# The division of the softmax rows moves from GpSimd to VectorE and ScalarE

## The chip, the core and the metric

One core of a Trainium2 chip runs the whole program. The metric is device microseconds of one execution. Engines are named as the profile names them: PE is TensorE's matrix multiply and PEld its weight load, DVE is VectorE, ACT is ScalarE, POOL is GpSimd, SP is SyncE, whose queue issues nearly all DMAs.

## The reference: causal attention, then two feed-forward layers

```python
scores = scale * np.matmul(q, k.transpose(0, 1, 3, 2))      # q, k, v: 2 x 12 x 448 x 64
scores = np.where(mask, -1000000000.0, scores)              # causal mask
scores = scores - np.max(scores, axis=-1, keepdims=True)
attn = np.exp(scores)
attn = attn / (np.sum(attn, axis=-1, keepdims=True) + 1e-09)
x = np.matmul(attn, v)                                      # -> 896 tokens x 768
h = x @ w_in1;  g = h * np.clip(h + 3.0, 0.0, 6.0) / 6.0;   x = g @ w_out1
h = x @ w_in2;  g = P(h) / (Q(h) + 1e-06);                  out = g @ w_out2
```

P is a cubic with coefficients a, Q is quadratic in |h| with coefficients b; the hidden width is 2048.

## The kernel before

**Attention stage.** The 24 heads are worked as 12 pairs: a pair is two heads of one batch, on the two halves of the 128 partitions. The 448 queries are cut into seven row blocks of 64, r = 0 to 6, and block r needs only (r + 1) * 64 columns of scores, so 1792 columns a pair. For each pair, in this order:

- *load, scores*: DMA of q and k, then 14 fp32 matmuls into four PSUM banks (line 427).
- *max*: DVE adds the mask and writes the scores to SBUF tile `e{r}` while it reduces the row extreme into `stat` (line 439, one per block).
- *exp*: ACT, in place on `e{r}`, with the row sum as accumulator (line 446).
- *bias, reciprocal*: DVE or ACT adds 1e-9 to the sums (lines 456 and 458), DVE takes the reciprocal (line 462). This is done for two parts of a pair: blocks 6, 5, 0 and blocks 4, 3, 2, 1.
- *norm*: `e{r}` is multiplied in place by its row's reciprocal (`a_norm`, lines 465 to 470). Before, GpSimd does all 84 of them.
- *transpose*: four groups of four 128x128 blocks of `e`, on PE with the identity, into one PSUM bank a group (line 476). A group needs the norms of the blocks it holds.
- *move*: the transposed bank is copied to SBUF tile `et` by ACT or DVE (lines 326 and 328).
- *apply*: `et` times `v` on PE (line 496). Then *x hi* (ACT, line 326) and *x rest* (DVE, line 508) split the result into two fp32r parts for the layers.

There are two sets of `e` tiles (`EB = 2`), so the maxima of pair n + 2 wait for the transposes of pair n; six `et` tiles and three `v` tiles.

**Layers.** Every weight matrix comes as 64-bit words and is decoded in chunks of three 128x128 tiles: *magnitude* and *tail* on ACT (lines 610 and 616), *shift* and *sign* on DVE (620 and 626), *w hi* on ACT (326), *w rest* on DVE (644). The products (line 715) are three matmuls for each tile and batch, 128x448; there are 2304 of them. They may start when the last pair's scores are done, and each needs the pairs of its own rows of x, so the first products lie among the last pairs' transposes. Some chunks are decoded early, kept in DRAM and fetched again.

**What sets the order.** Nothing is reordered on the chip: each engine takes its instructions in the order in which the program was written out, and waits at the head of its queue. That order is made when the program is built, by the class `Program`. `add` files an operation with its due time, what it reads and writes, and a cost for each engine that may do it; `order` then takes again and again the operation and engine that could begin first (ties by due time) and books the cost on that engine. The costs are formulas such as `c_pool`; `DUE` shifts the due time by the kind of operation; `PAIR` is the distance of two pairs' due times; `STAY` puts off a change of PE's tiling. They move no data, but they decide the order on every engine and, where an operation lists two engines, which of them does it.

Of the kernel before, what the change touches and what calls it, by code (L numbers as in the profile page):

```python
# [35 lines left out]
class Program:  # L36
# [15 lines left out]

    TILING = {"scores": "quarters", "apply": "columns"}
    DRAIN = 0.16
    STAY = 5.83

    def __init__(self, rings, banks, due):
        self.rings, self.banks, self.due = rings, banks, due
# [2 lines left out]
    def add(self, kind, at, engines, fn, *args, reads=(), writes=(), new=()):  # L61

        self.ops.append((kind, at, engines, fn, args, tuple(reads), tuple(writes), tuple(new)))

    def order(self):
# [44 lines left out]
        while can:  # L112
            best = None
            for n, t in can.items():
# [20 lines left out]
                for e, cost in ops[n][2].items():  # L135
                    mine = max(t[e], free[e], room), due[n] + self.STAY * turn, n, e, cost
                    if best is None or mine < best:
# [46 lines left out]
def c_act(n):  # L184
    return 0.051 + n / 1200


def c_dve(n):
    return 0.068 + n / 960


def c_pool(n):
    return 0.15 + n * 0.0021


def c_pe(n, passes):
    return passes * (0.0025 + n / 2400)

# [5 lines left out]
def c_mm(n, passes):  # L204
# [2 lines left out]


DUE = {
    "load": -89.1,  # L210
    "keep": 0.0,
    "fetch": -20.0,
    "load v": -0.1,
    "norm": 4.2,
    "scores": 10.5,
    "max": -10.7,
    "exp": 31.3,
    "bias": 13.8,
    "reciprocal": -27.8,
    "transpose": -38.3,  # L220
    "move": 7.4,
    "apply": 15.3,
    "x hi": -25.6,
    "x rest": 70.4,
    "constants": -8.8,
    "w load": -84.1,
    "magnitude": -7.3,
    "tail": -30.5,
    "shift": 17.2,
    "sign": -12.6,  # L230
    "w hi": 79.6,
    "w rest": -29.6,
    "product": 0.0,
    "relu": 8.8,
    "gate": 1.1,
# [17 lines left out]
    "out": -3.6,  # L253
    "store": 7.5,
}
PAIR = 5.9


def plan(KM, KF):
# [17 lines left out]
def tile_attention_moe_moe2(  # L277
# [235 lines left out]
    for n in range(len(pairs)):  # L513
        t, last = PAIR * n, n == len(pairs) - 1
        for which in ("kr", "qr"):
            raw = which, n
            add(
                "load", t, {"act" if n == 0 and which == "qr" else "dma": 1.26}, qk_load, which, n,
                writes=[raw], new=[(which, raw)],
            )  # L520
        add(
            "load v", t, {"dma": 0.9}, v_load, n, reads=[("empty", n % VB)], writes=[("v", n)],
            new=[("v", ("v", n))],
        )
        sc = [("sc", n, held) for held in BANKS]
        add(
            "scores", t, {"pe": 1.7}, a_scores, n, reads=[("kr", n), ("qr", n)],
            writes=sc + ["scored"] * last, new=[("s", key) for key in sc],
        )
        for late, r in enumerate(order):  # L530
            w, first, mine = (r + 1) * CP, late == 0, next(held for held in BANKS if r in held)
            add(
                "max", t + late, {"dve": c_dve(w)}, a_max, n, r,
                reads=[("sc", n, mine), "masks"] + [("stat", n)] * (not first)
                + [("m", n, mine[0])] * (r != mine[0]),
                writes=[("e", n, r), ("st", n, r), ("m", n, r)] + [("stat", n)] * first,
                new=[(f"e{r}", ("e", n, r))] + [("stat", ("stat", n))] * first,
            )
            add(
                "exp", t + late, {"act": 0.235 + c_act(w)}, a_exp, n, r, reads=[("stat", n)],  # L540
                writes=[("e", n, r), ("st", n, r)],
            )
        for part, held in enumerate((STRAIGHT, SWAPPED)):
            add(
                "bias", t + 2 * part, {"act": 0.2, "dve": 0.1}, a_bias, n, part,
                reads=[("st", n, r) for r in held] + [("stat", n)], writes=[("r", n, part)],
            )
            add(
                "reciprocal", t + 2 * part, {"dve": 0.15}, a_recip, n, part, reads=[("stat", n)],
                writes=[("r", n, part)],  # L550
            )
            for r in held:
                w = (r + 1) * CP
                add(
                    "norm", t + 2 * part, {"pool": c_pool(w)}, a_norm, n, r,
                    reads=[("r", n, part), ("stat", n)], writes=[("e", n, r)],
                )
        for g, group in enumerate(GROUPS):
            add(
                "transpose", t + g, {"pe": 0.436}, a_transpose, n, g,  # L560
                reads=["masks", ("pads", n % EB)] + [("e", n, r) for r in sorted({r for r, _ in group})],
                writes=[("pt", n, g)], new=[("t", ("pt", n, g))],
            )
            add(
                "move", t + g, {"act": c_act(512), "dve": c_dve(512)}, a_move, n, g,
                reads=[("pt", n, g)], writes=[("et", n, g)], new=[("et", ("et", n, g))],
            )
        for a, gs_ in enumerate(APPLY):
            cols = 1024 * len(gs_) // len(GROUPS)
            add(  # L570
                "apply", t + 2 * a, {"pe": c_pe(cols, 4) + 0.1}, a_apply, n, a,
                reads=[("et", n, g) for g in gs_] + [("v", n)], writes=[("o", n)],
                new=[("o", ("o", n))] if a == 0 else (),
            )
        b, hp = pairs[n]
        add("x hi", t, {"act": c_act(S) + 0.04}, a_hi, n, reads=[("o", n)], writes=[("x", hp, b)])
        add("x rest", t, {"dve": c_dve(S)}, a_lo, n, reads=[("o", n)], writes=[("x", hp, b)])
# [22 lines left out]
    raw, full, tail, split = {}, {}, {}, {}  # L600
# [54 lines left out]

    base = PAIR * len(pairs) + 10

# [208 lines left out]
    t, i, every = base, 0, tuple(range(B))  # L866
# [6 lines left out]
    while i < len(chunks):  # L873

        side = chunks[i][0][0] == 2
        n = 1 if not side else 2 if chunks[i + 2][0][0] == 2 else 3
# [72 lines left out]
```

## Time and profile before

| | |
|---|---|
| runs of the kernel | 560.67 us, median of 3 (560.19 to 560.8) |
| the profiled execution | 560.22 us, of which the span in the trace is 558.4 us |
| PE busy | 538.7 us (96%) |
| DVE, ACT, POOL busy | 423.2, 397.9 and 82.2 us |
| granted TensorE clock, mean | 0.991 of full speed |

The span is the time from the first to the last instruction; the rest of the device time lies around it. A busy share is an average over two stages that have different limits: the attention stage is roughly the first 100 us, the layers are the rest. Times in the trace count from the start of the span.

### The profile page before, as it was taken

How to read it: one execution, taken by the hardware profiler on the slowest of the kernel's cores; microseconds unless marked ns; L12 is line 12 of the kernel's file. 1: busy time of each engine (PE TensorE's matmuls, PEld its weight loads, DVE VectorE, ACT ScalarE, POOL GpSimd, SP SyncE). 2: the span in 40 equal slices, each digit the busy share in tenths (PEclk: the TensorE clock that was granted, in tenths of full speed). 3: DMA queues.
4: the chain of work that ended last, by engine and by line, in shares of the span. 5: the costliest groups of instructions: out<-in, count | busy, mean ns of one | idle time of the engine just before them, and what ended most of it. 6: DMA issues, size and time to landing. Idle time of an engine off the chain costs nothing.

```text
span 558.4 us, 9410 instructions
## 1 busy us (share of the span) xinstructions
PE 538.7 (96%) x3236; PEld 492.8 (88%) x3236; DVE 423.2 (76%) x925; ACT 397.9 (71%) x882; POOL 82.2 (15%) x104
## 2 busy tenths in 40 slices
PE   6888887999999999999999999999999999999997
PEld 5766766999999999999999999999999999999996
DVE  3588784679999998777777349999989999975420
ACT  5798885579898987776776359788678778855410
POOL 3999978000000000000000000000000000000000
PEclk9699999999999999999999999999999999999999
DMA  5775141147778777777766342234324323336100
GB/s 163 219 202 166 43 119 58 54 146 213 249 253 242 258 231 279 258 252 242 243 236 223 136 137 85 86 94 165 110 85 136 118 86 103 124 112 188 61 33 33
DMA packets 39311, 87.12 MB, mean 156 GB/s; under 512 B 4704, under 2 KB 14688, under 8 KB 39264
## 3 DMA queue, kind: packets, MB, share of 16 engines
q1 hardware_dynamic: 39104, 86.30, 47.9%
q8 instruction: 25, 0.41, 0.3%
q10 hardware_dynamic: 160, 0.23, 0.1%
q14 instruction: 22, 0.18, 0.1%
HBM read 71.18 MB, written 15.34 MB: 155 GB/s over the span
## 4 chain that ended last, share of the span: by engine, by line
PE 85%; POOL 11%; DVE 2%; issue 1%; ACT 1%; POOLq 0%; DVEq 0%
PE bank L715 82%; POOL e L470 11%; DVE e L439 1%; PE bank L476 1%; PE bank L376 1%; PE bank L496 1%; PE bank L427 1%; ACT et L326 0%; DVE et L328 0%; POOLq L945 0%; ACT e L446 0%; ACT o L326 0%; DVE stat L462 0%; ACT tail L616 0%; POOL ident masks.py:199 0%
## 5 line engine op out<-in xcount | busy, mean ns | idle before, releaser
L715 PE MATMUL bank<-yh,w 128*128 128x448 f32 x384 | 112.0, 362 | 0.0
L715 PE MATMUL bank<-rh,w 128*128 128x448 f32 x384 | 97.2, 362 | 0.0
L715 PE MATMUL bank<-xh,w 128*128 128x448 f32 x384 | 93.7, 363 | 0.0
L715 PE MATMUL bank<-ph,w 128*128 128x448 f32 x384 | 92.6, 362 | 0.0
L644 DVE TENSOR_TENSOR w<-full,w 128x384 fp32r<-128x384 f32 x96 | 53.2, 555 | 46.0 <-ACT w L326 45.6
L326 ACT ACTIVATE w<-full 128x384 fp32r<-128x384 f32 x96 | 50.2, 523 | 51.6 <-PE bank L715 50.8
L616 ACT ACTIVATE tail<-raw 128x384 uint32<-128x384 uint8 x128 | 69.4, 554 | 23.0 <-DVE full L620 19.7
L610 ACT ACTIVATE full<-raw 128x384 f32<-128x384 f32 x128 | 68.9, 549 | 20.2 <-DVE w L644 19.1
L620 DVE SCALAR_TENSOR_TENSOR full<-full,tail 128x384 uint32<-128x384 uint32 x128 | 69.7, 555 | 17.3 <-ACT full L610 15.5
L470 POOL TENSOR_SCALAR e<-e,stat 128x448 f32<-128x448 f32 (+6 forms) x84 | 79.5, 971 | 12.2 <-DVE stat L462 8.4
L715 PEld LDWEIGHTS bank<-rh,w 128*128 128x128 f32 x384 | 71.9, 188 | 5.2 <-ACT qy L783 0.3
L715 PEld LDWEIGHTS bank<-yh,w 128*128 128x128 f32 x384 | 71.9, 187 | 5.1 <-DVE p L767 0.5
L715 PEld LDWEIGHTS bank<-ph,w 128*128 128x128 f32 x384 | 72.0, 188 | 4.6
L715 PEld LDWEIGHTS bank<-xh,w 128*128 128x128 f32 x384 | 71.7, 188 | 4.5
L626 DVE SCALAR_TENSOR_TENSOR full<-raw,full 128x384 uint32<-128x384 uint32 x128 | 69.5, 558 | 1.9
L715 PE MATMUL bank<-yl,w 128*128 128x448 f32 x192 | 69.6, 363 | 0.0
L715 PE MATMUL bank<-rl,w 128*128 128x448 f32 x192 | 54.3, 362 | 0.0
L715 PE MATMUL bank<-xl,w 128*128 128x448 f32 x192 | 53.8, 361 | 0.0
L715 PE MATMUL bank<-pl,w 128*128 128x448 f32 x192 | 53.8, 361 | 0.0
L446 ACT ACTIVATE e<-e,stat 128x448 f32<-128x448 f32 (+6 forms) x84 | 41.7, 503 | 7.7 <-DVE stat L439 7.2
L476 PE MATMUL bank<-ident,e 128*128 128x128 f32 x192 | 28.5, 295 | 15.0 <-POOL e L470 15.0
L476 PEld LDWEIGHTS bank<-ident,e 128*128 128x128 f32 x192 | 22.4, 149 | 22.6 <-POOL e L470 22.4
(56 smaller groups left out, 732.9 us busy)
## 6 DMA issues: line engine op xcount, KB each, us to landing
raw<-in_w SPq DMA_DIRECT2D x128, 384.0 KB, 3.5
kept<-ws SPq DMA_DIRECT2D x32, 384.0 KB, 4.1
w<-kept SPq DMA_DIRECT2D x32, 384.0 KB, 3.3
kr<-in_kT SPq DMA_DIRECT2D x24, 112.0 KB, 2.9
out_T<-o SPq DMA_DIRECT2D x12, 224.0 KB, 2.2
qr<-in_qT SPq DMA_DIRECT2D x22, 112.0 KB, 2.9
v<-in_v SPq DMA_DIRECT2D x12, 128.0 KB, 2.8
v<-in_v SPq DMA_DIRECT2D x12, 96.0 KB, 3.0
```

The lines of the kernel that those rows point to most:

```text
L326: e.activation(out, in_, AF.Copy)
L376: e.matmul(bank[banks[0]][:, :P], ident, ident, start=True, stop=True)
L427: e.matmul(tiles["sc", n, r][halves[slot]], q[halves[j], r * CP:w], k[halves[j], :w], start=True, stop=True,)
L446: e.activation(t, t, AF.Exp, bias=stat[:, 0, at_:at_ + 1], scale=-1.0, accum_out=stat[:, 1, at_:at_ + 1],)
L470: e.tensor_scalar(t, t, by, None, ALU.mult)
L476: e.transpose(to[:, x], es[n % EB][r][:, c * P:(c + 1) * P], ident)
L610: e.activation(full[i], high, AF.Copy, scale=TO_F32)
L616: e.activation(tail[i], top, AF.Copy, bias=-31.0 / 64.0, scale=1.0 / 32.0)
L620: e.scalar_tensor_tensor(bits, bits, 3, tail.pop(i), ALU.logical_shift_left, ALU.bitwise_or)
L626: e.scalar_tensor_tensor(bits, raw.pop(i)[:, :, :, 1], 0x80000000, bits, ALU.bitwise_and, ALU.bitwise_or)
L644: e.tensor_tensor(split[i][:, 1], full.pop(i), split[i][:, 0], ALU.subtract)
L715: e.matmul(sums[which, m, b], split[i][:, w, j, :], x, start=k == 0 and n == 0, stop=last and n == 2,)
```

## The change

The operation *norm* may now be done by DVE or ACT, whichever the planner finds free first, and no longer by POOL. POOL keeps the masks, the identity and the zeros at the start. `a_norm` itself had both forms already: `activation` with a per-row scale on ACT, `tensor_scalar` elsewhere. Two costs of PE operations, `STAY`, `PAIR` and most numbers of `DUE` are other values; two lines of that table are shown.

```diff
-    STAY = 5.83
+    STAY = 2.21
...
+def c_norm(n, r, w):
+    return {"dve": 0.07 + w / 1920, "act": 0.06 + w / 1200}
...
-    "load": -89.1,
+    "load": -129.6,
...
-    "norm": 4.2,
+    "norm": 10.4,
...
-PAIR = 5.9
+PAIR = 5.6
...
-            "scores", t, {"pe": 1.7}, a_scores, n, reads=[("kr", n), ("qr", n)],
+            "scores", t, {"pe": 1.42}, a_scores, n, reads=[("kr", n), ("qr", n)],
...
-                    "norm", t + 2 * part, {"pool": c_pool(w)}, a_norm, n, r,
+                    "norm", t + 2 * part, c_norm(n, r, w), a_norm, n, r,
...
-                "apply", t + 2 * a, {"pe": c_pe(cols, 4) + 0.1}, a_apply, n, a,
+                "apply", t + 2 * a, {"pe": c_pe(cols, 4) + 0.08}, a_apply, n, a,
```

In the changed kernel's file every line from 196 on stands four lines lower: the norms are lines 472 (ACT) and 474 (DVE) there, the transposes 480, the products 719.

Counted over the whole program, DVE gets 46 of the 84 norms (4, 6, 7, 7, 9, 5 and 8 of the widths 448, 384, 320, 256, 192, 128 and 64: 11,008 columns) and ACT gets 38 (8, 6, 5, 5, 3, 7 and 4: 10,496 columns). The moves go from 27 on ACT and 21 on DVE to 16 and 32, and the additions of 1e-9 from 14 on ACT and 10 on DVE to 5 and 19. Every other operation stays on its engine.

ACT's queue at the first two pairs; tiles `e_91` to `e_97` are blocks 0 to 6 of the first set (pair 0), `e_98` to `e_104` those of the second (pair 1), and `stat` holds a pair's row numbers. Before:

```order
L446 ACTIVATE e_94,stat_196<-e_94,stat_196 128x256
L456 ACTIVATE stat_196<-stat_196 128x3
L446 ACTIVATE e_104,stat_214<-e_104,stat_214 128x448
L446 ACTIVATE e_92,stat_196<-e_92,stat_196 128x128
L446 ACTIVATE e_98,stat_214<-e_98,stat_214 128x64
L446 ACTIVATE e_102,stat_214<-e_102,stat_214 128x320
L446 ACTIVATE e_100,stat_214<-e_100,stat_214 128x192
L446 ACTIVATE e_103,stat_214<-e_103,stat_214 128x384
```

The same place in the changed kernel:

```order
L450 ACTIVATE e_94,stat_193<-e_94,stat_193 128x256
L450 ACTIVATE e_104,stat_214<-e_104,stat_214 128x448
L450 ACTIVATE e_92,stat_193<-e_92,stat_193 128x128
L450 ACTIVATE e_98,stat_214<-e_98,stat_214 128x64
L450 ACTIVATE e_102,stat_214<-e_102,stat_214 128x320
L472 ACTIVATE e_96<-e_96,stat_193 128x384
L472 ACTIVATE e_94<-e_94,stat_193 128x256
L472 ACTIVATE e_92<-e_92,stat_193 128x128
L450 ACTIVATE e_100,stat_214<-e_100,stat_214 128x192
```

Three norms of pair 0 stand between the exponentials of pair 1, and the addition of 1e-9 has left for DVE. DVE's queue a little later, where pair 0 is normalised and pair 2's first maximum follows. Before:

```order
L439 ISA e_99,stat_214<-bank_73,mask 128x128
L439 ISA stat_214 128x1
L458 TENSOR_SCALAR stat_196<-stat_196 128x4
L462 RECIPROCAL stat_196<-stat_196 128x4
L458 TENSOR_SCALAR stat_214<-stat_214 128x3
L462 RECIPROCAL stat_214<-stat_214 128x3
L328 COPY et_0_276<-bank_78 128x512
L439 ISA e_97,stat_281<-bank_74,mask 128x448
```

The same place in the changed kernel:

```order
L443 ISA e_99,stat_214<-bank_73,mask 128x128
L443 ISA stat_214 128x1
L466 RECIPROCAL stat_193<-stat_193 128x3
L466 RECIPROCAL stat_193<-stat_193 128x4
L474 TENSOR_SCALAR e_97<-e_97,stat_193 128x448
L474 TENSOR_SCALAR e_91<-e_91,stat_193 128x64
L474 TENSOR_SCALAR e_95<-e_95,stat_193 128x320
L474 TENSOR_SCALAR e_93<-e_93,stat_193 128x192
L332 COPY et_0_272<-bank_78 128x512
L443 ISA e_97,stat_279<-bank_74,mask 128x448
```

Four norms now stand ahead of the first move and of pair 2's maxima. PE's queue at the end of the attention stage, from the last transposes (line 476, now 480) on. Before:

```order
L476 MATMUL bank_76<-ident,e_101 128x2x64
L476 MATMUL bank_76<-ident,e_102 128x2x64 x2
L715 MATMUL bank_73<-xh_82,w_867 128x448
L715 MATMUL bank_78<-xh_84,w_867 128x448
L715 MATMUL bank_73<-xl_83,w_867 128x448
L715 MATMUL bank_78<-xl_85,w_867 128x448
L715 MATMUL bank_73<-xh_82,w_867 128x448
L715 MATMUL bank_78<-xh_84,w_867 128x448
L496 MATMUL bank_80<-et_0_1286,v_107 64x128 x4
```

The same place in the changed kernel:

```order
L480 MATMUL bank_78<-ident,e_101 128x2x64
L480 MATMUL bank_78<-ident,e_102 128x2x64 x2
L500 MATMUL bank_79<-et_0_1214,v_106 64x128 x4
L500 MATMUL bank_79<-et_1_1236,v_106 64x128 x2
L500 MATMUL bank_79<-et_1_1236,v_106 64x64 x4
L500 MATMUL bank_79<-et_2_1238,v_106 64x256 x2
L500 MATMUL bank_79<-et_3_1265,v_106 64x192 x2
L500 MATMUL bank_79<-et_3_1265,v_106 64x64 x2
L719 MATMUL bank_76<-xh_82,w_1104 128x448
```

The apply of pair 10 now stands behind the last transposes, with twelve products between it and the apply of pair 11, where there were six products and the apply of pair 11 alone. Ahead of the last transposes stand 30 products instead of 24.

## Rows read from the trace of the kernel before

**Rows 1.** The page's chain that ended last, share of the span by line

```profile
PE bank L715 82%; POOL e L470 11%; DVE e L439 1%; PE bank L476 1%; PE bank L376 1%; PE bank L496 1%; PE bank L427 1%; ACT et L326 0%; DVE et L328 0%; POOLq L945 0%; ACT e L446 0%; ACT o L326 0%; DVE stat L462 0%; ACT tail L616 0%; POOL ident masks.py:199 0%
```

**Rows 2.** Busy time in two stretches: its length, then each engine, clock and DMA

```profile
40.00:60.00 20.00, 17.35 (x236) 13.66 (x232) 17.19 (x64) 18.17 (x61) 19.68 (x21) 1.00 0.51 145
...
130.00:200.00 70.00, 70.00 (x352) 65.63 (x351) 67.18 (x135) 62.60 (x135) 0.00 (x0) 1.00 0.78 252
```

**Rows 3.** The page's group of the norms on POOL

```profile
L470 POOL TENSOR_SCALAR e<-e,stat 128x448 f32<-128x448 f32 (+6 forms) x84 | 79.5, 971 | 12.2 <-DVE stat L462 8.4
```

**Rows 4.** The chain in order of time, 0 to 130 us: start, length, what

```profile
11.57 5.75 POOL e L470 x6
...
88.38 6.83 POOL e L470 x7
...
95.25 1.09 PE bank L476 x8
96.34 1.21 PE bank L715 x6
97.55 1.91 PE bank L496 x32
99.46 30.61 PE bank L715 x152
```

**Rows 5.** Waits in 0 to 100 us: total, times, longest

```profile
PE bank L476 <- POOL e L470: 15.0, 15, 3.3
```

**Rows 6.** Timeline of the start: start, length, what [idle before <-releaser]

```profile
7.30 0.62 DVE L439 CUSTOM_DVE_ANT_0 e<-bank,mask 128x448 f32<-128x448 f32 x1 [7.30 <-PE bank L427]
...
7.97 0.67 ACT L446 ACTIVATE e<-e,stat 128x448 f32<-128x448 f32 x1 [5.97 <-DVE stat L439]
...
9.72 0.62 DVE L439 CUSTOM_DVE_ANT_0 e<-bank,mask 128x448 f32<-128x448 f32 x1
...
11.14 0.65 ACT L446 ACTIVATE e<-e,stat 128x448 f32<-128x448 f32 x1
...
11.79 0.39 ACT L446 ACTIVATE e<-e,stat 128x128 f32<-128x128 f32 x1
...
12.51 0.18 DVE L462 RECIPROCAL stat<-stat 128x4 f32<-128x4 f32 x1
...
14.25 1.97 PE L476 MATMUL bank<-ident,e 128*128 128x128 f32 x8 [3.31 <-POOL e L470]
```

**Rows 7.** ACT's groups by form, 0 to 97 us: count, busy us, mean ns

```profile
L326 ACT ACTIVATE et<-bank 128x512 f32<-128x512 f32 x27 | 15.4, 593 | 9.8 <-PE bank L476 9.8
...
L446 ACT ACTIVATE e<-e,stat 128x448 f32<-128x448 f32 x12 | 8.0, 666 | 6.2 <-DVE stat L439 6.0
...
L616 ACT ACTIVATE tail<-raw 128x384 uint32<-128x384 uint8 x10 | 5.6, 568 | 0.0
...
L446 ACT ACTIVATE e<-e,stat 128x64 f32<-128x64 f32 x12 | 4.0, 337 | 0.0
```

**Rows 8.** ACT's groups by form, 110 to 560 us

```profile
L778 ACT ACTIVATE qy<-qy,cabs 128x448 f32<-128x448 f32 x32 | 24.4, 763 | 0.0
...
L326 ACT ACTIVATE ph<-r 128x448 fp32r<-128x448 f32 x30 | 16.2, 577 | 0.0
```

**Rows 9.** ACT's timeline at two moves that stand back to back

```profile
89.12 1.09 ACT L326 ACTIVATE et<-bank 128x512 f32<-128x512 f32 x2 [1.38 <-PE bank L476]
```

**Rows 10.** DVE's groups by form, 0 to 97 us

```profile
L328 DVE COPY et<-bank 128x512 f32<-128x512 f32 x21 | 14.3, 689 | 10.6 <-PE bank L476 10.6
...
L508 DVE TENSOR_TENSOR xl<-bank,xh 128x448 fp32r<-128x448 f32 x11 | 6.8, 618 | 2.6 <-ACT xh L326 2.6
...
L644 DVE TENSOR_TENSOR w<-full,w 128x384 fp32r<-128x384 f32 x5 | 2.7, 553 | 0.0
...
L458 DVE TENSOR_SCALAR stat<-stat 128x3 f32<-128x3 f32 x5 | 0.9, 177 | 1.6 <-ACT e L446 1.5
```

**Rows 11.** Busy time in one stretch of the start; the clock stands behind POOL

```profile
14.00:17.20 3.20, 1.97 (x8) 1.57 (x8) 1.89 (x9) 2.00 (x9) 3.20 (x5) 0.50 0.67 180
```

More of the change, by code (lines that the diff above doesn't have):

```diff
@@ L209 @@
 DUE = {
-    "load": -89.1,
+    "load": -129.6,
     "keep": 0.0,
     "fetch": -20.0,
-    "load v": -0.1,
-    "norm": 4.2,
[L215 to L224, printed above, removed]
-    "constants": -8.8,
[L226 to L232, printed above, removed]
+    "load v": -6.0,
+    "norm": 10.4,
+    "scores": 82.3,
+    "max": 7.9,
+    "exp": 41.8,
+    "bias": 53.5,
+    "reciprocal": -23.1,
+    "transpose": -59.3,
+    "move": 79.1,
+    "apply": 17.6,
+    "x hi": -4.4,
+    "x rest": 64.7,
+    "constants": -8.8,
+    "w load": -65.6,
+    "magnitude": -11.0,
+    "tail": -25.2,
+    "shift": 108.9,
+    "sign": -47.0,
+    "w hi": 60.9,
+    "w rest": -8.8,
     "product": 0.0,
```

## The prediction

> **What bounds the kernel now.** I read the chain that ended last first. By line it is 82% products and 11% norms on POOL; all other lines are at 1% or less [rows 1]. The two belong to different stages. In the layers PE is busy for all of 130 to 200 us [rows 2], and the chain holds nothing but products from 99.46 on [rows 4]. So nothing that this change touches can be won there, and the question is when the layers' products can run without a break. In the attention stage the chain is a string of norms, from 11.57 to 88.38 + 6.83 = 95.21, then the last transposes, six products, the last apply, and products to the end [rows 4]. POOL's 84 norms are 79.5 us of work [rows 3] in those 83.64 us: the bound engine works 95% of the time, 6.97 us a pair. The other side of it is PE, which waited 15.0 us for norms ahead of transposes [rows 5]. In 40 to 60 us POOL was busy for 19.68 of 20, ACT for 18.17, PE for 17.35, DVE for 17.19 [rows 2]. That is the warning in this profile: ACT and DVE are not idle engines that could take 80 us of work for nothing.
>
> **What is fixed behind the last norm.** From 95.21 to the end of the span (558.4) are 463.2 us, and PE is the chain throughout. In the changed order six more products stand ahead of the last transposes (six take 1.21 [rows 4], so -1.2), but the apply of pair 10 now stands behind them (1.91 [rows 4], so +1.9). So the span after the change is the end of the last norm, call it T, + 463.9. T is what has to be found; now it is 95.21.
>
> **What the norms cost on ACT.** The nearest rows are the exponentials: same tile, same widths, in place, one per-partition operand. Their means are 666 ns for 448 columns and 337 for 64 [rows 7], so 0.282 us + 0.857 ns a column. Records overlap: a move's mean is 593 ns [rows 7], but two back to back take 1.09 [rows 9], so each costs 0.10 less than its record. 38 norms with 10,496 columns: 38 x 0.182 + 9.0 = 15.9 us. Bounds: a per-partition operand costs 93 ns (763 ns with two [rows 8] against 577 without, halved); if the norm had no such cost it would be 12.4, and without the overlap 19.7. I take 15.9, since the operand is there.
>
> **What ACT has to do until the last norm**, from its first exponential at 7.97 [rows 6]: the exponentials of pair 0 take 11.14 - 7.97 = 3.17 for six and one addition of 1e-9 (0.10), and 0.39 for the seventh [rows 6], so 3.46 a pair and 41.5 for twelve; the norms 15.9; 12 of the moves that are left to it, 0.49 each, 5.9; ten x hi of 448 columns at 0.45, 4.5; five additions, 0.5; 16 decoding steps at 0.47 (568 ns less the overlap [rows 7]), 7.5. Sum 75.8 us. What the planner put on ACT behind the last norm (4 moves, 2 x hi, 7 decoding steps) is covered by the 4.3 us of products and applies that PE does meanwhile, and by chunks that are decoded already.
>
> **What DVE has to do**, from 7.30 [rows 6]: seven maxima in 9.72 - 7.30 = 2.42 [rows 6], 29.0 for twelve pairs; 31 moves at 0.59 (689 ns less 0.10, the overlap taken from ACT [rows 10]), 18.3; ten x rest at 0.52, 5.2; 13 decoding steps at 0.45, 5.9; 43 additions and reciprocals at 0.08, 3.4. Sum 61.8 and the 46 norms. The trace has no wide tensor_scalar on DVE. Below, there is its fixed part, 0.08 by the 177 ns of the three-column one [rows 10]: 3.7. Above, there are the two-input steps, 553 ns for 384 columns and 618 for 448 [rows 10], so 1.02 ns a column: 46 x 0.063 + 11.2 = 14.1. Those are the nearest wide rows, so I take 14.1: 75.9 us in all, as much as ACT.
>
> The Trainium skill says otherwise of this operation: by "VectorE: DVE Perf Modes", the perf-mode tier table, an fp32 tensor_scalar from SBUF to SBUF runs at two columns a cycle. No run here shows it yet. By its figures (58 cycles and half a cycle a column at 0.96 GHz, an estimate) the 46 norms would be 8.5 us and DVE's sum 70.3. The forecast below goes by ACT and holds with either; the page only makes it likelier that DVE has room to spare.
>
> The skill also has a rule against half of this change: "ScalarE: Activation LUTs", Rules for kernel authors, would give a multiplication to VectorE and not to ScalarE. All 84 on DVE, at the price by the rows (38 x 0.063 + 10,496 x 1.02 ns = 13.1 more), would load DVE with 89.0 us and leave ACT with 60: T would be later than with the split.
>
> **The sum.** The bound engine now keeps 95% [rows 3, 4]. With the same for ACT, T = 7.97 + 75.8 / 0.95 = 87.8, against 95.21: 7.4 us earlier. At the start the gain is visible and small: ACT reaches the first norm after ten exponentials, at about 13.0, so that the first transposes start at 13.5 instead of 14.25 [rows 6]; pair 0 is normalised at about 14.3, where POOL needed until after 17.32 [rows 4]. After that a pair costs ACT 6.3 us / 0.95 = 6.6 instead of POOL's 6.97. The span is 87.8 + 463.9 = 551.7. The profiled execution had 560.22 us for a span of 558.4, and the median of the runs (560.67) lies 0.45 above it, so 2.2 us are to be added: **554.0 us**. POOL's empty queue costs and gives nothing more: what it still does is over before the first scores.
>
> PE is not the bound by then: 17.35 busy of 20 [rows 2] at 6.97 us a pair is 6.05 a pair. Even counted from 7.30, with 2.6 us of waiting at the start (its 3.31 ahead of 14.25 [rows 6], less 0.7), twelve pairs end at 82.5.
>
> **The rivals.**
>
> *ACT's norm is cheaper than the exponential* (12%). Without the 93 ns the sum is 72.3, T = 84.1, 550.2 us. For it speaks only that a plain copy may treat its scale differently; the two-operand row is against it.
>
> *Both engines are full at once and wait for each other* (12%). DVE at 75.9 and ACT at 75.8 are level; a move or a norm that is late on one holds up the next exponential or maximum on the other, since both queues are in order. Now, when neither is the bound, ACT is busy for 18.17 of 20 us, 91% [rows 2]. With 88% T is 94.1 and the time 560.2: no change. Against it: POOL's norms were waited for in the stretch that gave that 91%.
>
> *A pair's chain through two sets of tiles becomes the period: slower* (7%). The maxima of pair n + 2 wait for the transposes of pair n, so a period is half of the way from first maximum to last transpose. The norms now stand in two queues that also hold the exponentials and moves of other pairs. It decides from 14.0 us a chain on, twice the 7.0 us that would give T = 95.6 from 11.57 on. At 15 us T = 11.57 + 12 x 7.5 = 101.6 and the time 567.7. Against it: pair 0's chain should now be 7.30 to about 17.
>
> *PE's clock* (6%). The granted clock is 0.50, so 1.2 GHz, in 14 to 17.2 [rows 11], after PE had nothing to do for the 3.31 us up to 14.25 [rows 6], and 1.00 in 40 to 60 [rows 2]. The first transposes come only 0.7 us earlier, so it will fall again. PE has 5 us of room up to T; each us of low clock takes half a us of it. If the low clock lasted 14 us longer than now, T would be 89.8 and the time 555.9.
>
> *The layers wait for weights* (3%). DVE is 96% busy in 130 to 200 us [rows 2], and the chunks' due times moved too. PE has a ring of four chunks against it. 0.1 us for each of 128 chunks would be 12.8 us and take the whole gain: 566.8.
>
> **How the numbers follow.** The likeliest case, ACT as the bound, has 60%: 554.0, from 549.9 with no wait at all (T = 83.8) to 557.4 with 91%. With the rivals I give the range 548.5 to 560.0: the cheaper norm with fewer waits below, mutual waiting above. 0.2% is 1.1 us, about what a measurement of this kernel can tell from no change: faster means below 559.55, slower above 561.8. Faster: 60 + 12 + 6 and a third of the mutual waiting, 82%. Same: the rest of that and a little of the chain, 9%. Slower: chain and weights, 9%.
>
> **What would show it.** Right: POOL empty once its masks and zeros are made; the last norm at 87 to 89 us, PE's wait for norms well under 15.0 us, and ACT busy for over 19 of 20 us in the middle of the stage; ACT's norm at 0.67 us for 448 columns; products from the last apply to the end without a break. DVE's norm near 0.5 us for 448 columns would fit the rows (0.063 + 0.457). By the Trainium skill's table it would be near 0.3. Wrong: ACT and DVE both below 90% busy while PE waits for them (mutual waiting or the chain); a PE that is busy all through 25 to 85 (then the gain is larger than forecast); waits of products for weights after 100 us.

## The result, and the profile after

The changed kernel takes 554.62 us (median of 4 runs, 554.32 to 554.76), beside 560.43 for the kernel before on the same chip: a ratio of 0.9896, 95% interval 0.9879 to 0.9913. It is faster by 5.8 us. Its profiled execution took 554.57 us for a span of 552.8.

The page's chain that ended last, by line (L719 are the products, L450 the exponentials, L472 the norms on ACT):

```profile
PE bank L719 84%; ACT e L450 4%; ACT e L472 1%; PE bank L500 1%; PE bank L480 1%; DVE e L443 1%; DVE et L332 1%; PE bank L380 1%; DMA ca<-in_a 1%; ACT xh L330 0%; DVE xl L512 0%; ACT et L330 0%; SPq L398 0%; SPq L403 0%; SPq L404 0%
```

POOL's 11% [rows 1] have gone, ACT's exponentials and norms have 5% in their place, and a transfer stands in the chain that was not in it before, that of `ca`. The busy time by stretch (length, PE, PEld, DVE, ACT, POOL, then clock and DMA):

```profile
20.00:40.00 20.00, 17.08 (x200) 12.62 (x194) 15.96 (x71) 15.97 (x53) 0.00 (x0) 0.91 0.73 212
40.00:60.00 20.00, 19.39 (x250) 14.31 (x248) 19.43 (x81) 20.00 (x70) 0.00 (x0) 1.00 0.40 112
60.00:80.00 20.00, 19.09 (x229) 14.74 (x222) 19.80 (x73) 19.89 (x64) 0.00 (x0) 1.00 0.29 86
130.00:200.00 70.00, 70.00 (x352) 65.61 (x351) 66.63 (x133) 62.37 (x134) 0.00 (x0) 1.00 0.75 246
```

In 40 to 60 us POOL's 19.68 has become ACT's 20.00, and DVE and PE are close behind [rows 2]. In 20 to 40 both ACT and DVE stand for 4 us of 20. The layers, 130 to 200, are as before. The waits in 8 to 100 us (total, times, longest):

```profile
ACT cabs L597 <- DMA cb<-in_b: 4.0, 1, 4.0
DVE cneg L594 <- DMA ca<-in_a: 3.6, 1, 3.6
PE bank L480 <- ACT e L472: 3.3, 2, 2.8
```

PE's wait for norms went from 15.0 us [rows 5] to 3.3, nearly all of it the one ahead of the first transposes. The other two rows are one place in the program. `cabs` and `cneg` are small tables that the layers need after 100 us; the planner set their making early. Both stand in queues that run in order, and everything behind them waits. SP's queue shows why `ca` and `cb` came late (start, length, what):

```profile
16.72 1.23 SPq L398 DMA_DIRECT2D qr<-in_qT  x2
18.00 0.64 SPq L403 DMA_DIRECT2D v<-in_v  x1
...
21.97 0.60 SPq L590 DMA_DIRECT2D ca<-in_a  x1
22.62 0.43 SPq L591 DMA_DIRECT2D cb<-in_b  x1
23.10 0.43 SPq L608 DMA_DIRECT2D raw<-in_w  x1
```

SP needs 1.2 us for the two loads of one q or k, and it issues q and k up to pair 6 before the first v; `ca` goes out at 21.97, as the thirty-third transfer of that queue.

The end of the last norm, from DVE's timeline, and the chain in order of time (start, length, what):

```profile
87.61 0.28 DVE L474 TENSOR_SCALAR e<-e,stat 128x128 f32<-128x128 f32 x1
```

```profile
21.97 4.32 DMA ca<-in_a
...
78.33 2.48 PE bank L719 x11
...
87.50 1.22 PE bank L719 x6
88.72 1.31 PE bank L480 x12
...
96.46 33.60 PE bank L719 x167
```

`ca` took 4.32 us from the start of its issue to its reader, and its wait is a piece of the chain. T, the end of the last norm, is 87.89, the forecast 87.8; the rest of the span is 464.9, the forecast 463.9. But the chain does not pass through T. From 78.33, where an *x rest* on DVE lets it go on, PE never waits again, and the last transposes (88.72) start 0.83 us after the last norm, behind six products that follow PE's other work without a gap. The norms' price, from the groups by form in 0 to 100 us (count, busy us, mean ns):

```profile
L472 ACT ACTIVATE e<-e,stat 128x448 f32<-128x448 f32 x8 | 5.3, 664 | 0.0
...
L474 DVE TENSOR_SCALAR e<-e,stat 128x64 f32<-128x64 f32 x8 | 2.0, 244 | 0.0
L474 DVE TENSOR_SCALAR e<-e,stat 128x448 f32<-128x448 f32 x4 | 1.8, 452 | 0.0
...
L472 ACT ACTIVATE e<-e,stat 128x64 f32<-128x64 f32 x4 | 1.4, 344 | 0.0
```

ACT's norm is an exponential to within 7 ns (666 and 337 [rows 7]). DVE's grows by (452 - 244) / 384 = 0.54 ns a column.

### The profile page after: what moved, and what is told of

Its sections match the earlier page's. It is cut to its first block, busy times and chain, and to the rows that moved or that the text cites. A ratio compares the mean times of both kernels' runs of the same rounds, so it can differ in the third digit from the quotient of the medians.

```text
span 552.8 us, 9366 instructions
## 1 busy us (share of the span) xinstructions
PE 540.2 (98%) x3236; PEld 493.3 (89%) x3236; DVE 438.3 (79%) x991; ACT 405.8 (73%) x900; POOL 2.8 (1%) x20
## 4 chain that ended last, share of the span: by engine, by line
PE 87%; ACT 7%; DVE 3%; SPq 1%; DMA 1%; issue 1%; POOL 0%; POOLq 0%; ACTq 0%
PE bank L719 84%; ACT e L450 4%; ACT e L472 1%; PE bank L500 1%; PE bank L480 1%; DVE e L443 1%; DVE et L332 1%; PE bank L380 1%; DMA ca<-in_a 1%; ACT xh L330 0%; DVE xl L512 0%; ACT et L330 0%; SPq L398 0%; SPq L403 0%; SPq L404 0%
## 5 line engine op out<-in xcount | busy, mean ns | idle before, releaser
L719 PE MATMUL bank<-yh,w 128*128 128x448 f32 x384 | 112.6, 363 | 0.0
L719 PE MATMUL bank<-rh,w 128*128 128x448 f32 x384 | 96.9, 361 | 0.0
L719 PE MATMUL bank<-xh,w 128*128 128x448 f32 x384 | 94.3, 364 | 0.6 <-DVE xl L512 0.5
L719 PE MATMUL bank<-ph,w 128*128 128x448 f32 x384 | 92.6, 362 | 0.0
L624 DVE SCALAR_TENSOR_TENSOR full<-full,tail 128x384 uint32<-128x384 uint32 x128 | 70.0, 555 | 13.5 <-ACT full L614 12.2
L719 PEld LDWEIGHTS bank<-xh,w 128*128 128x128 f32 x384 | 71.6, 188 | 6.4 <-DVE xl L512 0.8
L719 PEld LDWEIGHTS bank<-yh,w 128*128 128x128 f32 x384 | 72.0, 188 | 5.1 <-DVE p L771 0.4
L719 PEld LDWEIGHTS bank<-ph,w 128*128 128x128 f32 x384 | 72.0, 188 | 5.0
L719 PEld LDWEIGHTS bank<-rh,w 128*128 128x128 f32 x384 | 71.9, 187 | 4.9
L630 DVE SCALAR_TENSOR_TENSOR full<-raw,full 128x384 uint32<-128x384 uint32 x128 | 68.3, 554 | 1.6
L719 PE MATMUL bank<-yl,w 128*128 128x448 f32 x192 | 69.2, 361 | 0.0
L719 PE MATMUL bank<-rl,w 128*128 128x448 f32 x192 | 54.6, 363 | 0.0
L719 PE MATMUL bank<-pl,w 128*128 128x448 f32 x192 | 53.9, 362 | 0.0
L719 PE MATMUL bank<-xl,w 128*128 128x448 f32 x192 | 53.8, 362 | 0.0
L450 ACT ACTIVATE e<-e,stat 128x320 f32<-128x320 f32 (+6 forms) x84 | 41.6, 499 | 6.2 <-DVE stat L443 6.2
L719 PEld LDWEIGHTS bank<-yl,w 128*128 128x128 f32 x192 | 35.9, 187 | 2.6
L719 PEld LDWEIGHTS bank<-rl,w 128*128 128x128 f32 x192 | 36.0, 188 | 2.3
L719 PEld LDWEIGHTS bank<-xl,w 128*128 128x128 f32 x192 | 36.0, 187 | 2.2
```

The source lines that it names most:

```text
L450: e.activation(t, t, AF.Exp, bias=stat[:, 0, at_:at_ + 1], scale=-1.0, accum_out=stat[:, 1, at_:at_ + 1],)
L624: e.scalar_tensor_tensor(bits, bits, 3, tail.pop(i), ALU.logical_shift_left, ALU.bitwise_or)
L630: e.scalar_tensor_tensor(bits, raw.pop(i)[:, :, :, 1], 0x80000000, bits, ALU.bitwise_and, ALU.bitwise_or)
L719: e.matmul(sums[which, m, b], split[i][:, w, j, :], x, start=k == 0 and n == 0, stop=last and n == 2,)
```

## The experiments

Two readings of the after trace had to be told apart. T came out as forecast, but the 5% of idle time that the forecast spread over the whole stage is one hole of 4 us at 22.5. **Theory A:** the hole is the loss, and without it the kernel is 4 us faster. **Its rival:** the hole hides another wait. In that stretch both engines would have had to wait for PE, whose first apply waits for `v` of pair 0 and whose clock falls again.

**1. Making the tables late.** Changed kernel, and the kernel before, with `cneg` and `cabs` put just ahead of their first use:

```diff
+        late = [x for x in plan if x[0][3].__name__ in ("c_neg", "c_abs")]
+        plan = [x for x in plan if x not in late]
+        at = next(n for n, x in enumerate(plan) if x[0][0] in ("abs", "affine"))
+        plan[at:at] = late
```

> The changed kernel with one edit: the two small operations on the rational's coefficients (cneg on DVE, cabs on ACT) stand just ahead of their first use in the layers and no longer in the attention stage; every other instruction keeps its order. In the changed kernel both engines stand at them from 22.7 to 26.3 us until the DMAs of the coefficients land. Theory A: DVE and ACT set the pace after 30 us, so that the 3.6 us are lost for good and come back: 551.0 us (550.5 to 552). Rival: in that stretch the engines would have had to wait for PE anyway (the first apply waits for the load of v until 21.6, the clock falls again), so that under 1 us comes back: 553.7 or more.

> The kernel before with the same edit. There the coefficients are waited for as well (ACT 0.8 us at 32 us), but POOL sets the pace of the stage. Theory A, that a wait counts only on the bound engine: no change, 560.4 within 0.5. Rival, that the small operations cost in any kernel of this shape: 1 us or more faster.

The changed kernel took 554.63 (0.9902, 0.9887 to 0.9916): not a tenth was won. The kernel before took 560.09 (0.9996, 0.9980 to 1.0012), as expected. Theory A falls in this form: the wait was there, it went, and the time stayed. The changed kernel's waits in that run, its first apply on PE, and its busy time in 22 to 26 us show where the hole went:

```profile
ACT xh L335 <- PE bank L505: 5.4, 2, 2.8
...
DVE et L337 <- PE bank L485: 4.0, 2, 3.5
...
ACT tail L625 <- DMA raw<-in_w: 2.1, 1, 2.1
```

```profile
21.73 3.25 PE L505 MATMUL bank<-et,v 128*64 128x128 f32 x32 [2.06 <-DVE stat L467]
```

```profile
22.00:26.00 4.00, 4.00 (x39) 3.59 (x36) 0.46 (x3) 0.74 (x3) 0.00 (x0) 0.57 0.36 77
```

The rival is what came. PE stood for 2.06 us ahead of the first apply and was then full for 4 us at a granted clock of 0.57, so mostly at 1.2 GHz, while ACT and DVE waited for it; behind that ACT stood for the first raw weights.

**2. Either part alone.** The norm on ACT and DVE with the old numbers, and the new numbers with the norm on POOL (the line exchanged, everything else of the changed kernel):

```diff
-                    "norm", t + 2 * part, c_norm(n, r, w), a_norm, n, r,
+                    "norm", t + 2 * part, {"pool": c_pool(w)}, a_norm, n, r,
```

> The kernel before with one part of the change alone: the norm may go to DVE or ACT by the same costs; STAY, PAIR, the due times and the two PE costs are those of before. Theory A, that the move of the norms makes the gain: at least 3 us faster than before, 552 to 557. Rival, that the new numbers make it: 559 or slower.

> The other part alone: the changed kernel's STAY, PAIR, due times and PE costs, with all norms on POOL at the old cost. Theory A: POOL's 80 us of norms bound the stage as before, the last norm ends at 94 to 98 us and the time is 559 to 564. Rival, that the new numbers make the gain: 557 or faster.

Measured: the norm alone 564.42 (1.0072, 1.0053 to 1.0092), slower than before; the numbers alone 562.93 (1.0049, 1.0034 to 1.0064), slower too. The first expectation failed and the second held. The windows of the first run show where the norm alone fails:

```profile
40.00:60.00 20.00, 16.50 (x210) 12.32 (x202) 16.10 (x68) 20.00 (x66) 0.00 (x0) 1.00 0.30 84
60.00:80.00 20.00, 17.27 (x212) 13.19 (x212) 17.12 (x67) 19.68 (x64) 0.00 (x0) 0.91 0.38 107
```

ACT is full while DVE (third) has 3 to 4 us of 20 to spare. With the old due times the planner put 50 norms of 13,184 columns and 25 moves on ACT, where the changed kernel has 38 of 10,496 and 12 until the last norm. By the prediction's prices that is 4.5 us of norms and 6.4 of moves more, less some 3 us of other steps: 83.5 us from 7.97, and with the 4.7 us for which ACT stood behind an apply that waited for `v`, 96.2. The last ACT norm ran from 96.75 to 97.25. So the sum over ACT's queue also tells, to 1 us, where this version's norms end.

That is not the whole loss. The last norm is 2.0 us later than before (95.21), but the profiled execution, the longest of its four with 566.93, is 6.7 us longer than that of the kernel before. The rest lies behind the norms, as this run's chain shows:

```profile
96.47 1.97 PE bank L480 x16
98.44 6.02 PE bank L719 x30
```

No product stands ahead of the last transposes here, where the kernel before has 24 and the changed kernel 30. At 1.21 us for six, 24 products are 4.8 us. So the numbers do two things: they share the work between ACT and DVE, and they give PE products to do among the last pairs. No run separates the two.

In the numbers-alone run PE waited for POOL 10.9 us (15.0 before). The gain is in neither part; it needs the norm's move and the numbers together.

**3. Which engine is full.** **Theory C**, as it was put before the runs: ACT, DVE and PE are level after 30 us, and each sets the pace in turn. By its rival for PE, PE, though 95 to 97% busy in 40 to 80 us, sets it from 78 us on only. Three runs add work that nothing else needs, once a pair: a copy of 0.48 us on ACT, an addition of 0.54 on DVE, a repeat of the first group of transposes on PE (0.42).

```diff
+        e.activation(junk, mask, AF.Copy)
...
+        e.tensor_tensor(junk, mask, mask, ALU.add)
...
-            e.transpose(to[:, x], es[n % EB][r][:, c * P:(c + 1) * P], ident)
+            for _ in range(2 if g == 0 else 1):
+                e.transpose(to[:, x], es[n % EB][r][:, c * P:(c + 1) * P], ident)
```

> The changed kernel, same order on every engine, with one operation more on ACT behind each pair's x hi: a copy of 448 columns from SBUF to a tile that nobody reads, about 0.48 us, twelve times, ten of them ahead of the last norm. Theory C, that ACT, DVE and PE are level after 30 us and each sets the pace in turn: 3 to 5 us slower than the changed kernel, 557.5 to 559.5. Rival, that ACT has room: under 556.

> The same with one operation more on DVE behind each x rest: an addition of 448 columns, about 0.54 us, ten of them ahead of the last norm. Theory C: 557 to 559.5. Rival, that ACT alone is the bound and DVE's 97% busy is padding that it can give up: under 556.

> The same with the first group of transposes of each pair done twice on PE (four transposes more, about 0.42 us a pair; same result). Theory C: 5 us of work more on an engine that is 97% busy from 40 to 80 us and the bound from 78 us on: 557.5 to 559.5. Rival, that ACT alone sets the pace up to 78 us: only the last four pairs count, 1.7 us, 556.3.

Measured: 558.24 with ACT's 5.8 us more (+3.6 to the changed kernel), 558.10 with DVE's 6.5 (+3.5), 555.80 with PE's 5.0 (+1.2). For ACT and DVE the theory held. For PE it failed (557.5 to 559.5 expected), and the rival came within 0.5 us: of its added work only that of the last four pairs, 1.7 us, was to count, 556.3. ACT and DVE each pass on over half of what is added, PE a quarter, though PE looked as busy (second column, of the PE run):

```profile
40.00:60.00 20.00, 19.65 (x257) 15.13 (x257) 19.45 (x83) 20.00 (x71) 0.00 (x0) 1.00 0.38 106
60.00:80.00 20.00, 19.84 (x236) 16.30 (x232) 19.80 (x74) 19.89 (x63) 0.00 (x0) 1.00 0.29 87
```

What ACT's and DVE's added work puts off is the point from which PE never waits again, 78.33 in the changed kernel. In the chains of their two runs, ACT's first:

```profile
81.97 2.48 PE bank L721 x11
```

```profile
81.63 2.48 PE bank L721 x11
```

The three differences are rough. In the profiles `cabs` ran at 26.92 and 27.06 us in the ACT and DVE runs and at 25.84 in PE's, instead of 26.49, so up to 0.6 us of each can be the hole's. PE's four runs spread from 554.80 to 556.34, and in its profile the granted clock in 20 to 40 us was 1.00 instead of 0.91; no run shows what that gave back. Up to 78 us the busy share of PE did not tell whether it had room; the added work did.

**4. One gate after the other.** If ACT and DVE are the bound, the hole at 22 us must cost its 4 us, and the first experiment contradicts that, unless something else of the start stops them at the same price. **Theory D:** it is `v` of pair 0, for which PE's first apply then waited. (The profile names a step of DVE as what ended that wait; the second half of `v` was issued at 18.82, and loads of `v` landed after 2.6 to 3.0 us, so at 21.4 to 21.8.) That load, two transfers, moved ahead of pair 3's k in SP's queue, on top of the late tables:

```diff
+        early = next(x for x in plan if x[0][0] == "load v")
+        plan.remove(early)
+        at = next(n for n, x in enumerate(plan) if x[0][0] == "load" and x[0][4] == ("kr", 3))
+        plan.insert(at, early)
```

> The changed kernel with the coefficients' two operations in the layers, as in e1_late_consts, and the load of the first pair's v ahead of the q and k of pair 3 in SP's queue; nothing else moves. With the coefficients late the time stayed, and the first apply still waited until 21.7 us, when v of pair 0 lands. Theory D, that this load is the gate of the start: v lands by 12 us, the first apply starts at 18 to 19 and 2 to 3 us come back: 551.5 to 552.8. Rival, that PE's low clock at the start or the pace of the three engines after it is the gate: 554 or more.

556.66 us (0.9929, 0.9909 to 0.9948): worse than the changed kernel by 2. Theory D falls. The first apply came 1.7 us earlier than in the first run, and ACT stopped at the next load of that queue:

```profile
28.06 0.54 ACT L629 ACTIVATE tail<-raw 128x384 uint32<-128x384 uint8 x1 [5.02 <-DMA raw<-in_w]
```

PE had little to do meanwhile, busy for 1.9 us of the six from 26 to 32, and its granted clock was 0.50 in 30 to 36. This profile is the fastest of six executions (555.55 to 557.84); why the others were slower still is not shown.

**Theory E:** each of `v`, the tables' inputs (`ca` and `cb`) and the first raw weights is a gate, one behind the other in SP's queue, and all have to be cleared at once. Moving the loads of pairs 5 and 6 (5.1 us of issuing, not needed before 45 us) behind the first raw weights was to do that; a second run moves pair 4's as well:

```diff
+        back = [x for x in plan if x[0][0] == "load" and x[0][4][1] in (5, 6)]
+        plan = [x for x in plan if x not in back]
+        at = next(n for n, x in enumerate(plan) if x[0][0] == "w load") + 1
+        plan[at:at] = back
```

> The changed kernel with one edit of SP's queue: the four loads of q and k of pairs 5 and 6 are issued behind the load of the first raw weights instead of ahead of the load of pair 0's v. In the changed kernel they take 5.1 us of SP's issuing (12.94 to 18.00) and are not needed before some 45 us, while v, the constants' inputs and the first raw weights, which stand behind them, are each waited for at 20 to 28 us. Now v is issued from 12.9, the constants' inputs from 16.9, the first raw weights from 18.0. Theory E (the start loses its 4 us of ACT and DVE to three gates of this queue in a row, and both engines are the level bound behind it, so clearing all three at once gives back what clearing one did not): ACT and DVE stand for under 1.5 us between 20 and 30 us, the last normalisation ends at 84 to 85.5, the span is 549.0 to 550.5, the time 550.5 to 552.3 us. Rival (some other wait of the start takes their place, PE at its low clock first of all, since two attempts to clear one gate each gave 0 and +2): 553.5 to 556 us, with ACT idle for 3 us or more at that place.

> As the kernel with the loads of pairs 5 and 6 issued behind the first raw weights, with those of pair 4 there too: v, the constants' inputs and the raw weights are issued another 3 us earlier. Theory E (all three gates are cleared by the smaller move already, and what remains is work of ACT and DVE): within 0.6 us of the smaller move, 550 to 552.3 us. Rival (the gates only bind earlier, each us of earlier issue gives something back): another 1 us or more below the smaller move. Second rival (PE at the low clock is the bound of the start): no better than the changed kernel, 553.5 to 556 us.

555.13 (0.9902, 0.9887 to 0.9917) and 554.69 (0.9899, 0.9883 to 0.9916): nothing won again. `cabs` now went through without a wait at 21.7, and ACT stopped 6 us behind it. ACT's timeline of the first of the two, and SP's at the load in question:

```profile
26.90 0.89 ACT L477 ACTIVATE e<-e,stat 128x448 f32<-128x448 f32 x2
32.73 0.54 ACT L625 ACTIVATE tail<-raw 128x384 uint32<-128x384 uint8 x1 [4.94 <-DMA raw<-in_w]
```

```profile
28.63 1.55 SPq L613 DMA_DIRECT2D raw<-in_w  x3
```

That is the second raw weights, issued at 28.63, where the changed kernel had them at 27.47. The edit had moved one gate and left the next where it was. So the mended theory names every load that ACT reaches before 35 us: the first four raw weights, which have buffers of their own, all go behind the tables' inputs, then pairs 5 and 6.

```diff
+        early = [x for x in plan if x[0][0] == "w load"][:4]
+        back = [x for x in plan if x[0][0] == "load" and x[0][4][1] in (5, 6)]
+        plan = [x for x in plan if x not in early + back]
+        at = next(n for n, x in enumerate(plan) if x[0][3].__name__ == "c_load") + 1
+        plan[at:at] = early + back
```

> The changed kernel with SP's queue in another order at the start: behind the constants' inputs come the loads of the first four raw weights, and only then those of q and k of pairs 5 and 6, which stood ahead of pair 0's v. In the two runs that moved only the first raw weights, ACT no longer stood for the constants at 22 us, but 4.0 and 4.9 us (28.1 and 27.8 on) for the second raw weights, which were issued at 28.3 to 28.6, no earlier than before. Theory E, mended (ACT and DVE together lose one stretch of some 4 us to whichever load of this queue comes next, and all of those that ACT reaches before 35 us must be issued ahead of q and k of pairs 5 and 6): the second to fourth raw weights are issued at 19 to 21 and landed by 26, ACT stands for under 1.5 us between 15 and 40 us, the last normalisation ends at 83 to 85.5, span 548 to 550.5, time 549.8 to 552.3 us. Rival 1 (a further wait takes the same 4 us again, as the v of pair 3, now issued behind more, or PE): 553.5 to 556. Rival 2 (the time of ACT and DVE was not the bound, PE is): ACT's wait goes, and its work stands later for PE in 60 to 90 us; 553 to 555.

550.88 us (five runs, 550.61 to 551.64), against 560.28 of before: 0.9836, 0.9821 to 0.9850. This version beats both kernels, by 9.4 and, over the runs of before beside each, 3.6 us. SP's queue and the windows:

```profile
18.08 1.85 SPq L614 DMA_DIRECT2D raw<-in_w  x4
```

```profile
20.00:40.00 20.00, 20.00 (x239) 14.48 (x232) 18.52 (x81) 19.12 (x65) 0.00 (x0) 0.97 0.73 221
40.00:60.00 20.00, 19.33 (x245) 14.27 (x244) 19.71 (x81) 20.00 (x67) 0.00 (x0) 1.00 0.48 132
60.00:80.00 20.00, 19.29 (x236) 15.79 (x233) 19.81 (x79) 19.88 (x65) 0.00 (x0) 1.00 0.25 76
```

ACT's 15.97 in 20 to 40 us has become 19.12; what is left of the hole is 0.88 us for `cb`. The last norm ends at 83.63, and the stretch in which PE never waits for ACT or DVE begins 4.25 us earlier than in the changed kernel:

```profile
74.08 2.48 PE bank L725 x11
```

In 40 to 80 us ACT is full; in 20 to 40 PE is as well (20.00), so that stretch is not ACT's alone.

**5. One norm in seven back on GpSimd**, on top of that version: the block of 320 columns of every pair goes to POOL.

```diff
+        plan = [
+            (x, "pool" if x[0] == "norm" and x[4][1] == 4 else e, banks) for x, e, banks in plan
+        ]
```

> The kernel with the first four raw weights issued ahead of q and k of pairs 5 and 6, with one of the seven normalisations of every pair (the one of 320 columns) given back to GpSimd, in the same order otherwise: 7 leave DVE and 5 leave ACT, 0.3 and 0.45 us each, 2.1 and 2.3 us of either engine's work. In the kernel before, GpSimd took 1154 ns for this block and stood for nothing but the 84 of them; now it stands for 93% of the time and can start each at once when its reciprocal is there. Theory C (ACT and DVE, level with each other, set the time, and GpSimd was late only because it had all seven): the last normalisation ends 1 to 2 us earlier than 83.6, the span is 547 to 548.5, the time 548.5 to 550.3 us. Rival (the transposes, whose third group needs this block, now wait for the 1.15 us of GpSimd and ACT and DVE wait behind PE): PE waits for GpSimd 3 us or more in all, 551 to 554 us.

551.08 us (0.9823, 0.9795 to 0.9851), no different from the 550.88 without it, and neither expectation holds: no gain, and PE hardly waited for POOL. DVE's groups by form, of the version without and the one with GpSimd's norm:

```profile
L480 DVE TENSOR_SCALAR e<-e,stat 128x192 f32<-128x192 f32 x9 | 2.8, 313 | 0.0
...
L480 DVE TENSOR_SCALAR e<-e,stat 128x448 f32<-128x448 f32 x4 | 1.8, 454 | 0.0
```

```profile
L483 DVE TENSOR_SCALAR e<-e,stat 128x192 f32<-128x192 f32 x9 | 3.8, 424 | 0.0
...
L483 DVE TENSOR_SCALAR e<-e,stat 128x448 f32<-128x448 f32 x4 | 1.8, 453 | 0.0
```

The same nine norms of 192 columns took 1.0 us more. Those of 448 columns, which ran clear of POOL's but for one that had begun before it, took the same. Over all forms DVE's norms went from 15.6 us (46) to 15.2 (39), though 2.7 us of them had left. One place where the two stand side by side, from DVE's and POOL's timelines:

```profile
47.60 1.08 POOL L483 TENSOR_SCALAR e<-e,stat 128x320 f32<-128x320 f32 x1 [5.08 <-DVE stat L475]
47.71 0.53 DVE L483 TENSOR_SCALAR e<-e,stat 128x192 f32<-128x192 f32 x1
```

0.53 us for 0.31. Not every DVE norm beside one of GpSimd's pays. GpSimd's first norm and the two that DVE began while it ran (count, busy us, mean ns):

```profile
12.31 1.20 POOL L483 TENSOR_SCALAR e<-e,stat 128x320 f32<-128x320 f32 x1 [8.79 <-DVE stat L475]
```

```profile
L483 DVE TENSOR_SCALAR e<-e,stat 128x64 f32<-128x64 f32 x1 | 0.5, 522 | 0.0
L483 DVE TENSOR_SCALAR e<-e,stat 128x192 f32<-128x192 f32 x1 | 0.3, 306 | 0.0
```

The one that began first took 522 ns instead of 246; the second took its usual 306. ACT's share was won (85.4 busy in 0 to 100 us against 86.8), DVE's was not, and with the two level that decides. No run tried a POOL norm that never meets one on DVE, so this cause is read from the records, not shown by an experiment of its own.

## Why the prediction was right, and where it was not

**The bound and the sum: right up to 78 us.** From the first exponential (8.23 in this profile) to the last norm (87.89) are 79.7 us, of which ACT stood 4.0; the remaining 75.7 answer to the forecast's 75.8. The first exponential starts between 7.2 and 8.2 from profile to profile, so the closeness of T is worth no more than about half a us. With the hole all but gone, 7.23 to 83.63 less 0.88 is 75.5. The forecast's floor, no wait at all, was T = 83.8 and 549.9; the measured version has 83.63 and 550.88.

**From T to the end: the number came by luck.** The prediction let T decide when the last transposes start, as it did before. After the change PE is the chain from 78.33 on, and the last transposes come when PE's own work ahead of them is done. ACT and DVE had 9.6 us of work left to T at that point, PE 10.4 to those transposes; that the two are so close is what makes the rest 464.9 beside 463.9, and the sum had no term for it. What ACT's and DVE's work sets is the start of that stretch: 78.33 here, 81.97 and 81.63 with work added, 74.08 without the hole.

**The 95%: right as a number, by luck, and wrong as a mechanism.** It was taken from POOL's share before, as if waiting were spread evenly. ACT was full from 28 to 68 us, and the missing 5% was one gate of SP's queue. The prediction read the queues of ACT and DVE and not SP's beside them. In the kernel before `cabs` waited 0.8 us, POOL's lateness covered it, and the step that takes `v`, `ca` and the weights into account was left out: nothing in the text asked what, once POOL was out of the way, was late next at the start.

**ACT's norm: right** (664 ns against the 0.67 forecast; three back to back took 1.29 us where their means make 1.50, so an overlap of about 0.1 is right too). The rival of a cheaper norm falls by the same row.

**DVE's norm: too dear by the rows.** Forecast 14.1 us for 46; their records sum to 15.6, and four in a row took 1.14 where their means make 1.39, so 0.083 overlap each and 11.8 remain. The slope of the nearest wide rows, 1.02 ns a column, was twice the measured 0.54; the fixed part was twice too small. Neither of the two signs given for 448 columns came: 0.45 us in the record, 0.37 without the overlap, for near 0.5 or near 0.3. The Trainium skill's page "VectorE: DVE Perf Modes", the perf-mode tier table, gave two columns a cycle: the trace agrees on the slope (an estimate of 0.52 ns by its figures) and not on the prediction's sum by that page, 8.5 us, since the fixed part is larger. The forecast time went by ACT's sum, so this term did not enter it.

**Levelness.** "As much as ACT" was said of 75.9 and 75.8, and with 2.3 us less on DVE it still held well enough: adding work to either cost nearly the same. The rival built on it, mutual waiting with 88%, did not come: both were over 97% busy in 40 to 80 us.

**PE: not the bound up to 78 us, as forecast, and the bound from there on, which was not.** The prediction had PE done with twelve pairs at 82.5, 5 us ahead of T. 5.0 us of added transposes cost 1.2, near the 1.7 that fall on the last four pairs. The sign that the text gave for the opposite, PE busy all through 25 to 85, does not tell the two stretches apart: PE was 95 to 97% busy in 40 to 80 with room left, and full behind.

**The clock.** The rival asked for 14 us more of low clock; this did not come. The granted clock was low twice for a short time, once as in [rows 11] and once behind the hole. It was 0.50, so 1.2 GHz, in 14 to 17 and in 28 to 30; in the second stretch DVE and ACT were full all the same:

```profile
14.00:20.00 6.00, 5.52 (x48) 4.96 (x52) 5.08 (x24) 5.95 (x23) 0.00 (x0) 0.75 0.63 182
...
28.00:32.00 4.00, 4.00 (x34) 2.28 (x28) 4.00 (x17) 4.00 (x16) 0.00 (x0) 0.67 0.99 291
```

**The layers did not wait for weights:** 70.00 of 70 us, as before. The chain of two buffers did not become the period. The start came as forecast, first transposes at 13.87 (13.5) instead of 14.25 [rows 6].

**Not foreseen at all:** that the norm's move without the new numbers would be slower than before. The diff's table of numbers looked like a re-tuning beside the change; it is the half that makes the other half pay, and part of that is the 24 or 30 products that it places ahead of the last transposes.

## What to carry to other kernels

When a bound engine is relieved, add up the work of each engine that takes over and look for the first wait in the queue of whoever feeds them: the sum forecast T to a tenth, but 4 us of it were a transfer of 2 KB issued as the thirty-third of its queue. Then ask which engine is the chain behind the last of that work: here PE was, from 78 us on, and T decided nothing more. Clearing one gate of an in-order queue proves nothing if the next stands right behind it; four runs that left one standing won nothing, and the fifth, which cleared all but 0.88 us, won 3.6 us. An idle engine need not be a free one: beside GpSimd's norms some of DVE's took longer.

## What the runs showed of the hardware that was not expected

A GpSimd norm can slow a DVE norm. One of 192 columns took 0.53 us while a GpSimd norm ran beside it and 0.31 alone, but of the two that DVE began beside the GpSimd norm of 12.31 the first took 0.52 us for 64 columns (0.25 alone) and the second its usual 0.31 for 192. Whether DVE slows GpSimd is not shown: GpSimd's block of 320 columns took 1.22 us in the mean, beside 1.15 in the kernel before, where DVE worked beside it too. The Trainium skill's "SBUF — State Buffer", section "Who interferes with whom", has such a rule: it says that a DVE instruction in a two-port mode and a GpSimd instruction cannot run together, and that the one that issues second is blocked until the first ends. The trace agrees that they collide and not that the second is fully blocked: the DVE norm at 47.71 ended at 48.24, 0.44 us before the GpSimd norm at 48.68.
